# Attention with a gated dense branch: the gate, its product with the accumulator and the last additions on GpSimd, and 122 heads with V stationary

## The chip, the cores and the metric

The kernel runs on one core of a Trainium2 chip. The time is device microseconds of one execution; the median of the runs is what two kernels are compared by. A separate execution was recorded by the hardware profiler, and the profile page and every row below come from that one. The engines are called PE (TensorE matmuls), PEld (its weight loads), ACT (ScalarE), DVE (VectorE), POOL (GpSimd) and SP (SyncE, which only issues DMAs here).

## The reference

```python
def _A_ref(x, k_cache, v_cache, wq, wo):
    B, Sq, D = x.shape                     # 1, 2048, 512
    H, Dh = 32, 128
    q = (x @ wq).reshape(B, Sq, H, Dh).transpose(0, 2, 1, 3)
    scores = jnp.einsum("bhqd,bhkd->bhqk", q, k_cache) * (Dh ** -0.5)   # 2048 keys
    p = softmax(scores, axis=-1)
    o = jnp.einsum("bhqk,bhkd->bhqd", p, v_cache)
    return o.transpose(0, 2, 1, 3).reshape(B, Sq, H * Dh) @ wo
...
xn = layernorm(x)
s = A(xn)
g = silu(relu(xn @ w1 + b1) ** 2 @ w2 + b2)     # hidden width 1792
return x + s * g
```

Everything that enters and leaves is bf16.

## The kernel before, in words

The 2048 query rows are cut into four blocks `j` of 512 rows. A block has 32 heads, so there are 128 passes, called heads here and numbered `g` = 0 to 127. One head takes eight steps (`pi`); in each step PE makes two 128-key score tiles of 512 columns in PSUM (`psA`, two buffers), ACT takes their exponential into `pT` (one 128x1024 instruction, a ring of `NPT` = 8 buffers), and two steps later PE multiplies `pT` with V into `psO`.

There are two forms of that second product. **P stationary** (`gen_pv`, line 1004): `pT` is loaded as weights and V is streamed, with a column of ones beside it that yields the softmax denominator: 64 matmuls of 129 columns in a head. DVE copies the result out (`o_un`), POOL scales it (`o_bf`, line 1061), and a transposing DMA puts it into `oT`. **V stationary** (`gen_pv_b`, line 756): V is loaded as weights and `pT` is streamed: 16 matmuls of 512 columns. The result is already turned round; ACT copies it out (`o_col`), and the denominator has to be summed apart. For each of the eight tiles of a head either DVE reduces the whole 128x1024 tile (`den_part`, line 775), or POOL first adds its halves into `h_sum` (`part_add`, line 788) and DVE reduces the 128x512 sum (`part_half`, line 796). Then come a small sum, a turn, a DMA out and back (`d_scr`, `d_quad`), a small sum and a reciprocal, a DMA out and a broadcast back (`r_scr`, `r_all`), and POOL multiplies `o_col` with it into `oT` (`den_scale`, line 856). `at_a` (line 448) lists the heads with P stationary: the first `FIRST_B`, the last three and those in `A_HEADS`, together 11; the other 117 have V stationary.

Beside the heads PE works through jobs in the `psF` banks, spread evenly over the steps (`fill_one`): the projections of later heads (evicted as `qt_sb`), the dense branch (`job_h`, evicted as `r_t` and `h2T`; `job_o2`, line 1147), and the output projection in chunks of eight heads (`job_wo`, line 1186), whose first chunks are summed in `acc`. The gate of a tile of 128 rows is made in steps: DVE adds `b2` (`z_t`), ACT takes tanh (`th_t`), DVE makes (tanh + 1) * z (`g_all`, line 1166). Before the last chunk, DVE multiplies `acc` with the gate (`acc_gate`, line 1247) and POOL adds x (`acc_add`, line 1254). At the last chunk DVE multiplies its product by the gate into `tmp_t` (which is `z_t`, line 408), DVE adds `acc` to it, and POOL issues the store of the row tile.

A planner in the program fixes the order of each engine's instructions beforehand from estimated costs (`_cost`, line 60). Pieces of DVE work are queued in `quiet` by due step and put in where DVE is expected free (`fill_dve`, line 944); `pool_quiet` is the like for POOL: what is ready first goes first (`fill_pool`, line 961). POOL is also given a `part_add` where DVE owes more than `POOL_OWED` ns of queued work. The engines then run these orders and wait for each other by semaphores. Line numbers of the profile are those of the one-line helpers (line 226 is the plain matmul, 231 the one for P stationary, 239 `_tt`, 249 `_stt`, 286 the turning reduce). The two softmax buffers are joined by this rule in `gen_scores`, which makes ACT wait for the denominator work:

```python
deps=[t, t_PV[pi - NPT] if pi >= NPT else None, t_part.get(pi - NPT)])
```

Of the kernel before, what the change touches and what calls it, by code (L numbers as in the profile page):

```python
# [59 lines left out]
def _cost(name, fn):  # L60
    f, k = fn.func, fn.keywords
    n = _elements(k["out"])
    if name == "PE":
        return n / 2.4 + 2.5, n / 2.4 + 166
    if name == "ACT":
        return n * 0.83 + 70, n * 0.83 + 172
    if name == "POOL":
        if f is _tt and n > 1:
            c = n * 2.3 + 55 if k["out"].tensor.name == "oT" else n * 2.05 + 60
            return c, c + 50  # L70
        return (500, 560) if f is _tt else (n + 100, n + 150)
    if f is _reduce_t:
        n = _elements(k["in_"])
    elif f is _reduce:
        n = _elements(k["in_"]) * 1.3 + 35
    elif f is _recip:
        n = n * 3.1
    elif f in (_bn_stats,):
        n = _elements(k["in_"])
    elif f is _ts and _in_sbuf(k["in0"]):  # L80
        n = n / 2
    return n / 0.96 + 70, n / 0.96 + 150


def _uses_port(name, fn):
    f, k = fn.func, fn.keywords
    if name == "POOL":
        return f in (_tt, _ts)
    if name == "DVE":
        if f in (_tt, _stt):  # L90
            return _in_sbuf(k["in0"]) and _in_sbuf(k["in1"])
        if f in (_ts, _copy):
            return _in_sbuf(k.get("in0", k.get("in_")))
    return False
# [206 lines left out]
def bass_recurrent_scan__mha_block_cached__dense_activation_squared_relu__prompt_kernel(  # L301
# [37 lines left out]
    LATE_EVICT = 250  # L339
    POOL_ROOM = 300  # L340
    SLACK = 1500
    FIRST_B = 3
    A_HEADS = (10, 31, 41, 64, 96)
    POOL_OWED = 3500
    HALF_SLACK = 600
    VW = 136

# [31 lines left out]
    o_col = sb("o_col", [P, NOC, QB], F32)  # L379
    h_sum = sb("h_sum", [P, NHS, QB], F32)  # L380
    rden = sb("rden", [P, 2, TPB], F32)
    o_bf = sb("o_bf", [P, 2, TPB, Dh], BF16)
    NBK = QB // 32
    d_part = sb("d_part", [P, 2, 2 * NPR, NBK], F32)
    d_sum = sb("d_sum", [P, 2, 32], F32)
# [5 lines left out]
    r_scr = nc.dram_tensor("r_scr", [2, QB], F32, kind="Internal").ap()  # L391
    r_t = sb("r_t", [P, 2, QB], BF16)
    z_t = sb("z_t", [P, 2, D], F32)
    th_t = sb("th_t", [P, 1, D], BF16)
    b1b = sb("b1b", [NFC, P], BF16)
    b1f = sb("b1f", [P, NFC], F32)
    b2bc = sb("b2bc", [P, D], BF16)
# [492 lines left out]
    def needs(fn):  # L890
        f, a = fn.func, fn.args
        if f in (den_part, part_half):
            m = b_no[a[0] // NPR]
            if m >= 2 and m - 2 not in t_sum:
                return None
            return [t_exp[a[0]]] if f is den_part else [t_part[a[0]]]
        if f in (den_sum, den_turn, den_write, den_read, den_total, den_recip, rec_write,
                 rec_read, den_scale):
            g = a[0]
            m = b_no[g]  # L900
            if f is den_sum and tiles[g] < NPR:
                return None
            first, before = {
                den_sum: (t_parts.get(g, []), t_row), den_turn: ([t_sum.get(m)], t_dw),
                den_write: ([t_row.get(m)], t_dr), den_read: ([t_dw.get(m)], t_tot),
                den_total: ([t_dr.get(m)], t_rw), den_recip: ([t_tot.get(m)], {}),
                rec_write: ([t_rec.get(m)], t_spr), rec_read: ([t_rw.get(m)], t_scale),
                den_scale: ([t_col.get(m), t_spr.get(m)], {})}[f]
            if m >= 2 and f not in (den_recip, den_scale):
                first = first + [before.get(m - 2)]  # L910
            return first
        if f is norm_recip:
            return t_oev[a[0]]
        if f is norm_scale:
            return [t_rden.get(a_no[a[0]])]
        if f is acc_gate:
            return [t_acc[a[1]], t_g.get(a[0] * TPB + a[1])]
        if f is acc_add:
            jt = a[0] * TPB + a[1]
            return [t_ug.get(jt), tok_xt.get(jt)]  # L920
        if f is ln_bn:
            return [t_xl.get(a[0] * TPB + a[1])]
        if f is ln_rstd:
            return [t_bn.get(a[0] * TPB + a[1])]
        if f is ln_next:
            return [t_xr.get(a[0] * TPB + a[1])]
        return gate_needs[fn]

    def ready_at(fn):
# [131 lines left out]
    def norm_scale(g):  # L1061
        m = a_no[g]
        base = rden[:, m % 2, :]
        rb = bass.AP(tensor=base.tensor, offset=base.offset,
                     ap=[list(base.ap[0]), [1, TPB], [0, Dh]])
        t_norm[m] = t_onorm[g] = E(
            GP if g < NG - 3 else DV, partial(_tt, out=o_bf[:, m % 2, :, :], in0=o_un[:, :, 0:Dh], in1=rb, op=ALU.mult),
            deps=[t_rden[m], t_obf[m % 2]])
        gen_oT(g)

    def gen_oT(g):
        tok_oT[g] = t_obf[a_no[g] % 2] = S.emit_dma(
            SP, partial(_dmaT, out=oT[:, g % NOT, :].rearrange("p (t q) -> p t q", q=P),
                        in_=o_bf[:, a_no[g] % 2, :, :].rearrange("p t d -> p (t d)")), sl_oT[g % 4],
            deps=[t_onorm[g], t_wodone[g - NOT] if g >= NOT else None])


# [69 lines left out]
    def job_o2(j, qt):  # L1147
# [11 lines left out]
        def evac(bank, step):  # L1159
            s = jt % 2  # L1160
            assert jt < 1 or jt - 1 in t_g
            tz = E(DV, partial(_tt, out=z_t[:, s, :], in0=bankF(bank), in1=b2bc[:], op=ALU.add),
                   deps=[t_o2[j, qt], tok_b2, t_zrd[s], t_tmp[s]])
            box = [None]

            def gate():
                gs = jt % TPB
                t_g[jt] = t_zrd[s] = t_thr[0] = E(
                    DV, partial(_stt, out=g_all[:, gs, :], in0=th_t[:, 0, :], scalar=1.0,
                                in1=z_t[:, s, :], op0=ALU.add, op1=ALU.mult),  # L1170
                    deps=[box[0], t_fin.get(jt - TPB)])

            def tanh():
                box[0] = E(AC, partial(_act, out=th_t[:, 0, :], in_=z_t[:, s, :], func=ACT.Tanh,
                                       scale=0.5), deps=[tz, t_thr[0]])
                fn = partial(gate)
                gate_needs[fn] = [box[0]]
                calm(step + 8, fn)

            at(step + 1, tanh)  # L1180
            return tz
        return NFC, mm, evac

    t_fin = {}

    def job_wo(j, m, qt, c0=0, c1=D):
        jt = j * TPB + qt
# [15 lines left out]
        def evac(bank, step):  # L1203
# [2 lines left out]
                    t_wodone[j * H + h] = box[0]  # L1206
            place = (bankF(bank) if isinstance(bank, int) else bank[0])[:, 0:c1 - c0]
            if m == 0:
                t_acc[qt] = t = E(DV, partial(_copy, out=acc[:, qt, :], in_=place),
                                  deps=[box[0], t_fin.get(jt - TPB)])  # L1210
            elif not last:
                t_acc[qt] = t = E(DV, partial(_tt, out=acc[:, qt, :], in0=place,
                                              in1=acc[:, qt, :], op=ALU.add),
                                  deps=[box[0], t_acc[qt]])
            if m == len(CH[j]) - 2:
                calm(step + 16, partial(acc_gate, j, qt))
                pool_quiet.append(partial(acc_add, j, qt))
            if last:
                s = jt % 2
                assert all(x in t_g for x in t_o2j)  # L1220
                t = E(DV, partial(_stt, out=tmp_t[:, s, c0:c1], in0=place, scalar=0.5,
                                  in1=g_all[:, jt % TPB, c0:c1], op0=ALU.mult,
                                  op1=ALU.mult),
                      deps=[box[0], t_g[jt], t_tmp[s], t_zrd[s]])
                end = jt >= NQB * TPB - 2
                row = (x_t if end else out_t)[:, s, c0:c1]
                eng = GP if j == NQB - 1 and qt in (0, 2) else DV
                t_fin[jt] = t_tmp[s] = E(
                    eng, partial(_tt, out=row, in0=tmp_t[:, s, c0:c1],
                                 in1=acc[:, qt, c0:c1], op=ALU.add),  # L1230
                    deps=[t, t_u[jt], None if end else t_outdma[s]])
                eng, sl = (SP, sl_fin) if j == NQB - 1 else (GP, sl_out)
                dma = S.emit_dma(
                    eng, partial(_dma, out=out[0, jt * P:(jt + 1) * P, c0:c1],
                                 in_=row), sl[s], deps=[t_fin[jt]])
                if c1 == D:
                    t_outdma[s] = dma
            return t
        return nh, mm, evac

    def load_xt(jt):
        if jt < NQB * TPB:
# [3 lines left out]

    def acc_gate(j, qt):
        jt = j * TPB + qt
        t_ug[jt] = E(DV, partial(_stt, out=acc[:, qt, :], in0=acc[:, qt, :], scalar=0.5,
                                 in1=g_all[:, jt % TPB, :], op0=ALU.mult, op1=ALU.mult),  # L1250
                     deps=[t_acc[qt], t_g[jt]])


# [115 lines left out]
                                        in_=bass.AP(tensor=B_b2.tensor, offset=B_b2.offset,  # L1369
                                                    ap=[[0, P], [1, D]])), sl_b2)  # L1370

    at(62, load_b2)
    for i in range(2):
        at(140 + 8 * i, partial(load_xt, i))
    tok_w2 = None
# [175 lines left out]
```

The softmax here doesn't subtract the row's maximum and nothing guards it: scores larger than these inputs give would overflow.

## Time and profile before

| | before |
|---|---|
| median of 4 runs | 1219.08 us (1219.01 to 1220.62) |
| the profiled execution, own time | 1219.09 us |
| its span | 1217.3 us |
| PE busy | 1212.2 us, 100% of the span, 6269 matmuls |
| ACT busy | 1090.5 us, 90% |
| DVE busy | 1067.2 us, 88% |
| POOL busy | 1064.2 us, 87% |
| granted TensorE clock | 1.0 throughout |

The span runs from the first instruction to the last; the 1.8 us that are missing to the execution's own time lie around it. A row of the groups reads: line, engine, operation, output<-inputs, shapes and types, count | busy us, mean ns of one | idle time of the engine just before, and who ended it. Matmuls overlap in the profile, so the mean ns of one matmul is not what it adds; the distance from one start to the next is.

### The profile page before, as it was taken

Reading aid. Unit: us, or ns where it says so; the run is one execution under the profiler, and the core shown is the slowest. Engines: PE = TensorE matmul, PEld = TensorE weight load, DVE = VectorE, ACT = ScalarE, POOL = GpSimd, SP = SyncE. Lnnn points to the kernel's source line nnn. Section 1 sums busy time; section 2 is a strip of 40 time slices with the busy share of each in tenths; the row PEclk is TensorE's granted clock in tenths of the full one; section 3 lists DMA queues with packets and bytes.
Section 4 is the critical chain, followed back from the end, with each engine's and each line's share of the span. In section 5 each row is a group of like instructions: output and inputs, shape, how many; then the busy total and the mean of one; then the engine's idle time right before and its main releaser. Section 6 shows DMA issues by size and latency. Waiting matters only on the chain.

```text
span 1217.3 us, 19831 instructions
## 1 busy us (share of the span) xinstructions
PE 1212.2 (100%) x6269; PEld 667.7 (55%) x6269; DVE 1067.2 (88%) x1865; ACT 1090.5 (90%) x1162; POOL 1064.2 (87%) x982
## 2 busy tenths in 40 slices
PE   9999999999999999999999999999999999999999
PEld 7555555555555555555555555555555555555556
DVE  4798889899999898879999999888999999889973
ACT  7898989999899898999989999999999999989995
POOL 1687999999898899999888899999998889999981
PEclk9999999999999999999999999999999999999999
DMA  9889787878788776776777777877667777777771
GB/s 214 178 197 223 185 182 168 192 167 182 180 158 177 170 162 155 165 159 153 169 160 165 169 168 166 163 163 165 162 163 167 167 164 164 155 165 161 160 154 49
DMA packets 510009, 203.47 MB, mean 167 GB/s; under 512 B 421808, under 2 KB 493744, under 8 KB 509904
## 3 DMA queue, kind: packets, MB, share of 16 engines
q1 hardware_dynamic: 507808, 198.13, 75.0%
q0 software_dynamic: 1424, 3.81, 1.1%
q8 instruction: 50, 0.82, 0.3%
q14 instruction: 55, 0.45, 0.1%
q10 hardware_dynamic: 672, 0.26, 0.1%
HBM read 128.23 MB, written 4.25 MB: 109 GB/s over the span
## 4 chain that ended last, share of the span: by engine, by line
PE 96%; DVE 2%; POOL 1%; ACT 0%; DMA 0%; issue 0%; ACTq 0%
PE psA L226 36%; PE psO L226 32%; PE psF L226 25%; PE psO L231 3%; DVE d_part L286 1%; DVE acc L249 1%; POOL h_sum L239 0%; ACT pT L235 0%; PE psA L231 0%; DMA x_ln<-in_A_x_dram 0%; DVE qt_sb L253 0%; POOL oT L239 0%; POOL acc L239 0%; DVE acc L239 0%; ACT kT L235 0%
## 5 line engine op out<-in xcount | busy, mean ns | idle before, releaser
L235 ACT ACTIVATE pT<-psA 128x1024 bf16<-128x1024 f32 x1025 | 1036.6, 1025 | 108.3 <-PE psA L226 72.3
L239 POOL TENSOR_TENSOR h_sum<-pT 128x512 f32<-128x512 bf16 x758 | 863.0, 1166 | 63.0 <-DVE d_part L286 31.1
L226 PE MATMUL psA<-qt_sb,kT 128*128 128x512 bf16 x2032 | 605.4, 380 | 0.4 <-ACT pT L235 0.4
L226 PE MATMUL psO<-pT,v_sb 128*128 128x512 bf16 x1872 | 556.8, 379 | 0.0
L286 DVE TRANSPOSE_TENSOR_REDUCE d_part<-h_sum 128x16 f32<-128x512 f32 x758 | 495.3, 678 | 17.8 <-POOL h_sum L239 17.1
L226 PEld LDWEIGHTS psA<-qt_sb,kT 128*128 128x128 bf16 x2032 | 285.5, 144 | 179.2 <-ACT pT L235 4.5
L226 PEld LDWEIGHTS psO<-pT,v_sb 128*128 128x128 bf16 x1872 | 183.1, 98 | 220.1 <-issue 0.6
L286 DVE TRANSPOSE_TENSOR_REDUCE d_part<-pT 128x32 f32<-128x1024 bf16 x178 | 215.4, 1213 | 12.1 <-ACT pT L235 11.4
L226 PE MATMUL psF<-xnT,wq_sb 128*128 128x512 bf16 (+1 forms) x520 | 168.8, 374 | 0.2 <-DVE xnT L253 0.2
L226 PE MATMUL psF<-wo_all,oT 128*128 128x512 bf16 x480 | 163.7, 379 | 0.0
L239 POOL TENSOR_TENSOR oT<-o_col,r_all 128x512 bf16<-128x512 f32 x117 | 150.1, 1283 | 12.2 <-DMA r_all<-r_scr 12.0
L253 DVE CAST qt_sb<-psF 128x512 bf16<-128x512 f32 (+1 forms) x130 | 87.1, 670 | 32.4 <-PE psF L226 30.1
L226 PE MATMUL psF<-xnT,w_sb 128*128 128x512 bf16 x224 | 77.6, 379 | 0.0
L226 PEld LDWEIGHTS psF<-xnT,wq_sb 128*128 128x128 bf16 x520 | 50.3, 98 | 45.9 <-issue 0.3
L226 PE MATMUL psF<-w_sb,h2T 128*128 128x512 bf16 x224 | 73.8, 379 | 0.0
L235 ACT ACTIVATE o_col<-psO 128x512 f32<-128x512 f32 x117 | 69.3, 592 | 0.0
L226 PEld LDWEIGHTS psF<-wo_all,oT 128*128 128x128 bf16 x480 | 46.9, 98 | 40.1
L231 PEld LDWEIGHTS psO<-v_sb,pT 128*128 128x128 bf16 x704 | 46.6, 98 | 19.0 <-ACT pT L235 0.4
L245 DVE TENSOR_SCALAR r_t<-psF,b1f 128x512 bf16<-128x512 f32 x56 | 41.5, 741 | 16.9 <-PE psF L226 15.5
L231 PE MATMUL psO<-v_sb,pT 128*128 128x129 bf16 x704 | 54.0, 220 | 0.1
L282 DVE TENSOR_REDUCE d_sum<-d_part 128x16 f32<-128x144 f32 (+3 forms) x117 | 46.2, 395 | 1.3
L249 DVE SCALAR_TENSOR_TENSOR h2T<-psF,b1f,r_t 128x512 bf16<-128x512 f32 x56 | 41.8, 746 | 1.7
(66 smaller groups left out, 376.0 us busy)
## 6 DMA issues: line engine op xcount, KB each, us to landing
v_sb<-in_A_v_cache_dram SPq DMA_DIRECT2D x508, 128.0 KB, 2.7
r_all<-r_scr SPq DMA_DIRECT2D x117, 256.0 KB, 3.8
wq_sb<-in_A_wq_dram SPq DMA_DIRECT2D x127, 128.0 KB, 3.1
wo_all<-in_A_wo_dram SPq DMA_DIRECT2D x16, 256.0 KB, 3.6
kT<-in_A_k_cache_dram SPq DMA_TRANSPOSE x254, 3.6
w_sb<-in_B_w_dram SPq DMA_DIRECT2D x14, 256.0 KB, 3.5
x_t<-in_A_x_dram POOLq DMA_DIRECT2D x16, 128.0 KB, 3.0
d_scr<-d_row SPq DMA_DIRECT2D x117, 16.0 KB, 2.5
```

The source lines that it names most:

```text
L226: return e.matmul(out, lhsT, rhs, start=start, stop=stop)
L231: return e.matmul(out, lhsT, rhs, start=start, stop=stop, skip_group_check=True)
L235: return e.activation(out, in_, func, bias=bias, scale=scale)
L239: return e.tensor_tensor(out, in0, in1, op)
L245: return e.tensor_scalar(out, in0, scalar1=scalar1, scalar2=scalar2, op0=op0, op1=op1)
L249: return e.scalar_tensor_tensor(out=out, in0=in0, scalar=scalar, in1=in1, op0=op0, op1=op1)
L253: return e.tensor_copy(out, in_)
L282: return e.tensor_reduce(out, in_, axis=AX.X, op=ALU.add)
L286: return e.tensor_reduce(out, in_, axis=AX.X, op=ALU.add, apply_transpose=True)
```

## The change

Four things change. (1) The gate, its product with `acc`, and, outside the last block of rows, the addition of `acc` at the last chunk move from DVE to POOL and to its queue `pool_quiet`; the gate becomes two instructions. `finish` is new and also issues the store. (2) The factors 0.5 go: `z_t` is halved as it is made and `b2` once at the start; `th_t` becomes f32. (3) `FIRST_B` and `A_HEADS` change so that only heads 0, 1, 64 and the last three have P stationary: 6 of them, and 122 with V stationary. (4) `POOL_OWED` goes from 3500 to 4000, `o_bf` has one buffer, and the planner's costs know the new instructions.

```diff
--- before.py
+++ after.py
@@ -65,8 +65,8 @@
     if name == "ACT":
         return n * 0.83 + 70, n * 0.83 + 172
     if name == "POOL":
-        if f is _tt and n > 1:
-            c = n * 2.3 + 55 if k["out"].tensor.name == "oT" else n * 2.05 + 60
+        if f in (_tt, _stt) and n > 1:
+            c = n * 2.3 + 55 if k["out"].tensor.name in ("oT", "out_t") else n * 2.05 + 60
             return c, c + 50
         return (500, 560) if f is _tt else (n + 100, n + 150)
     if f is _reduce_t:
@@ -85,7 +85,7 @@
 def _uses_port(name, fn):
     f, k = fn.func, fn.keywords
     if name == "POOL":
-        return f in (_tt, _ts)
+        return f in (_tt, _ts, _stt)
     if name == "DVE":
         if f in (_tt, _stt):
             return _in_sbuf(k["in0"]) and _in_sbuf(k["in1"])
@@ -339,9 +339,9 @@
     LATE_EVICT = 250
     POOL_ROOM = 300
     SLACK = 1500
-    FIRST_B = 3
-    A_HEADS = (10, 31, 41, 64, 96)
-    POOL_OWED = 3500
+    FIRST_B = 2
+    A_HEADS = (64,)
+    POOL_OWED = 4000
     HALF_SLACK = 600
     VW = 136
 
@@ -379,7 +379,7 @@
     o_col = sb("o_col", [P, NOC, QB], F32)
     h_sum = sb("h_sum", [P, NHS, QB], F32)
     rden = sb("rden", [P, 2, TPB], F32)
-    o_bf = sb("o_bf", [P, 2, TPB, Dh], BF16)
+    o_bf = sb("o_bf", [P, 1, TPB, Dh], BF16)
     NBK = QB // 32
     d_part = sb("d_part", [P, 2, 2 * NPR, NBK], F32)
     d_sum = sb("d_sum", [P, 2, 32], F32)
@@ -391,7 +391,7 @@
     r_scr = nc.dram_tensor("r_scr", [2, QB], F32, kind="Internal").ap()
     r_t = sb("r_t", [P, 2, QB], BF16)
     z_t = sb("z_t", [P, 2, D], F32)
-    th_t = sb("th_t", [P, 1, D], BF16)
+    th_t = sb("th_t", [P, 1, D], F32)
     b1b = sb("b1b", [NFC, P], BF16)
     b1f = sb("b1f", [P, NFC], F32)
     b2bc = sb("b2bc", [P, D], BF16)
@@ -924,6 +924,9 @@
             return [t_bn.get(a[0] * TPB + a[1])]
         if f is ln_next:
             return [t_xr.get(a[0] * TPB + a[1])]
+        if f is finish:
+            jt = a[0]
+            return [fin_needs[fn], t_u.get(jt), t_outdma[jt % 2]]
         return gate_needs[fn]
 
     def ready_at(fn):
@@ -1064,14 +1067,14 @@
         rb = bass.AP(tensor=base.tensor, offset=base.offset,
                      ap=[list(base.ap[0]), [1, TPB], [0, Dh]])
         t_norm[m] = t_onorm[g] = E(
-            GP if g < NG - 3 else DV, partial(_tt, out=o_bf[:, m % 2, :, :], in0=o_un[:, :, 0:Dh], in1=rb, op=ALU.mult),
-            deps=[t_rden[m], t_obf[m % 2]])
+            GP if g < NG - 3 else DV, partial(_tt, out=o_bf[:, 0, :, :], in0=o_un[:, :, 0:Dh], in1=rb, op=ALU.mult),
+            deps=[t_rden[m], t_obf[0]])
         gen_oT(g)
 
     def gen_oT(g):
-        tok_oT[g] = t_obf[a_no[g] % 2] = S.emit_dma(
+        tok_oT[g] = t_obf[0] = S.emit_dma(
             SP, partial(_dmaT, out=oT[:, g % NOT, :].rearrange("p (t q) -> p t q", q=P),
-                        in_=o_bf[:, a_no[g] % 2, :, :].rearrange("p t d -> p (t d)")), sl_oT[g % 4],
+                        in_=o_bf[:, 0, :, :].rearrange("p t d -> p (t d)")), sl_oT[g % 4],
             deps=[t_onorm[g], t_wodone[g - NOT] if g >= NOT else None])
 
 
@@ -1159,29 +1162,36 @@
         def evac(bank, step):
             s = jt % 2
             assert jt < 1 or jt - 1 in t_g
-            tz = E(DV, partial(_tt, out=z_t[:, s, :], in0=bankF(bank), in1=b2bc[:], op=ALU.add),
+            assert jt < 2 or not {x for x in fin_due if x % 2 == s}
+            tz = E(DV, partial(_stt, out=z_t[:, s, :], in0=bankF(bank), scalar=0.5, in1=b2bc[:],
+                               op0=ALU.mult, op1=ALU.add),
                    deps=[t_o2[j, qt], tok_b2, t_zrd[s], t_tmp[s]])
             box = [None]
 
             def gate():
                 gs = jt % TPB
+                assert jt < TPB or jt - TPB in t_fin
+                t = E(GP, partial(_tt, out=th_t[:, 0, :], in0=th_t[:, 0, :], in1=z_t[:, s, :],
+                                  op=ALU.mult), deps=[box[0]])
                 t_g[jt] = t_zrd[s] = t_thr[0] = E(
-                    DV, partial(_stt, out=g_all[:, gs, :], in0=th_t[:, 0, :], scalar=1.0,
-                                in1=z_t[:, s, :], op0=ALU.add, op1=ALU.mult),
-                    deps=[box[0], t_fin.get(jt - TPB)])
+                    GP, partial(_tt, out=g_all[:, gs, :], in0=th_t[:, 0, :],
+                                in1=z_t[:, s, :], op=ALU.add),
+                    deps=[t, t_fin.get(jt - TPB)])
 
             def tanh():
-                box[0] = E(AC, partial(_act, out=th_t[:, 0, :], in_=z_t[:, s, :], func=ACT.Tanh,
-                                       scale=0.5), deps=[tz, t_thr[0]])
+                box[0] = E(AC, partial(_act, out=th_t[:, 0, :], in_=z_t[:, s, :], func=ACT.Tanh),
+                           deps=[tz, t_thr[0]])
                 fn = partial(gate)
                 gate_needs[fn] = [box[0]]
-                calm(step + 8, fn)
+                pool_quiet.append(fn)
 
             at(step + 1, tanh)
             return tz
         return NFC, mm, evac
 
     t_fin = {}
+    fin_due = set()
+    fin_needs = {}
 
     def job_wo(j, m, qt, c0=0, c1=D):
         jt = j * TPB + qt
@@ -1206,6 +1216,7 @@
                     t_wodone[j * H + h] = box[0]
             place = (bankF(bank) if isinstance(bank, int) else bank[0])[:, 0:c1 - c0]
             if m == 0:
+                assert jt < TPB or jt - TPB in t_fin
                 t_acc[qt] = t = E(DV, partial(_copy, out=acc[:, qt, :], in_=place),
                                   deps=[box[0], t_fin.get(jt - TPB)])
             elif not last:
@@ -1213,30 +1224,41 @@
                                               in1=acc[:, qt, :], op=ALU.add),
                                   deps=[box[0], t_acc[qt]])
             if m == len(CH[j]) - 2:
-                calm(step + 16, partial(acc_gate, j, qt))
+                pool_quiet.append(partial(acc_gate, j, qt))
                 pool_quiet.append(partial(acc_add, j, qt))
             if last:
                 s = jt % 2
                 assert all(x in t_g for x in t_o2j)
-                t = E(DV, partial(_stt, out=tmp_t[:, s, c0:c1], in0=place, scalar=0.5,
-                                  in1=g_all[:, jt % TPB, c0:c1], op0=ALU.mult,
-                                  op1=ALU.mult),
+                assert not {x for x in fin_due if x % 2 == s}
+                t = E(DV, partial(_tt, out=tmp_t[:, s, c0:c1], in0=place,
+                                  in1=g_all[:, jt % TPB, c0:c1], op=ALU.mult),
                       deps=[box[0], t_g[jt], t_tmp[s], t_zrd[s]])
-                end = jt >= NQB * TPB - 2
-                row = (x_t if end else out_t)[:, s, c0:c1]
-                eng = GP if j == NQB - 1 and qt in (0, 2) else DV
-                t_fin[jt] = t_tmp[s] = E(
-                    eng, partial(_tt, out=row, in0=tmp_t[:, s, c0:c1],
-                                 in1=acc[:, qt, c0:c1], op=ALU.add),
-                    deps=[t, t_u[jt], None if end else t_outdma[s]])
-                eng, sl = (SP, sl_fin) if j == NQB - 1 else (GP, sl_out)
-                dma = S.emit_dma(
-                    eng, partial(_dma, out=out[0, jt * P:(jt + 1) * P, c0:c1],
-                                 in_=row), sl[s], deps=[t_fin[jt]])
-                if c1 == D:
-                    t_outdma[s] = dma
+                fn = partial(finish, jt, c0, c1, t)
+                if j == NQB - 1:
+                    finish(jt, c0, c1, t)
+                else:
+                    fin_due.add(jt)
+                    fin_needs[fn] = t
+                    pool_quiet.append(fn)
             return t
         return nh, mm, evac
+
+    def finish(jt, c0, c1, t):
+        s = jt % 2
+        end = jt >= NQB * TPB - 2
+        row = (x_t if end else out_t)[:, s, c0:c1]
+        eng = DV if jt >= NQB * TPB - TPB and s else GP
+        t_fin[jt] = t_tmp[s] = E(
+            eng, partial(_tt, out=row, in0=tmp_t[:, s, c0:c1], in1=acc[:, jt % TPB, c0:c1],
+                         op=ALU.add),
+            deps=[t, t_u[jt], None if end else t_outdma[s]])
+        eng, sl = (SP, sl_fin) if jt >= NQB * TPB - TPB else (GP, sl_out)
+        dma = S.emit_dma(
+            eng, partial(_dma, out=out[0, jt * P:(jt + 1) * P, c0:c1], in_=row), sl[s],
+            deps=[t_fin[jt]])
+        if c1 == D:
+            t_outdma[s] = dma
+        fin_due.discard(jt)
 
     def load_xt(jt):
         if jt < NQB * TPB:
@@ -1246,8 +1268,8 @@
 
     def acc_gate(j, qt):
         jt = j * TPB + qt
-        t_ug[jt] = E(DV, partial(_stt, out=acc[:, qt, :], in0=acc[:, qt, :], scalar=0.5,
-                                 in1=g_all[:, jt % TPB, :], op0=ALU.mult, op1=ALU.mult),
+        t_ug[jt] = E(GP, partial(_tt, out=acc[:, qt, :], in0=acc[:, qt, :],
+                                 in1=g_all[:, jt % TPB, :], op=ALU.mult),
                      deps=[t_acc[qt], t_g[jt]])
 
 
@@ -1369,7 +1391,13 @@
                                         in_=bass.AP(tensor=B_b2.tensor, offset=B_b2.offset,
                                                     ap=[[0, P], [1, D]])), sl_b2)
 
-    at(62, load_b2)
+    def halve_b2():
+        nonlocal tok_b2
+        tok_b2 = E(DV, partial(_ts, out=b2bc[:], in0=b2bc[:], scalar1=0.5, scalar2=None,
+                               op0=ALU.mult), deps=[tok_b2])
+
+    at(58, load_b2)
+    at(66, halve_b2)
     for i in range(2):
         at(140 + 8 * i, partial(load_xt, i))
     tok_w2 = None
```

## The prediction

> **What bounds the kernel now.** I read the page from the chain that ended last, then the stages, then the waits. The chain gives PE 96%; the stages say whether PE is full everywhere.
>
> ```profile
> PE 96%; DVE 2%; POOL 1%; ACT 0%; DMA 0%; issue 0%; ACTq 0%
> ```
>
> Busy time of each engine in stretches (the columns are the stretch, its length, then busy us of PE, PEld, DVE, ACT, POOL, with instructions in brackets):
>
> ```profile
> 60.00:90.00 30.00, 30.00 (x141) 15.97 (x139) 28.60 (x52) 27.33 (x29) 26.92 (x26) 1.00 0.89 197
> 600.00:630.00 30.00, 29.57 (x183) 17.13 (x182) 28.77 (x46) 25.78 (x28) 24.21 (x23) 1.00 0.74 158
> 990.00:1020.00 30.00, 30.00 (x141) 15.99 (x139) 28.98 (x54) 27.32 (x30) 26.43 (x25) 1.00 0.69 158
> ```
>
> From 30 to 1200 us PE is busy without a hole in every 30 us stretch except 600:630, which lacks 0.43 us. It does 140 to 141 matmuls of 512 columns in 30 us, so 0.2155 us each (696 in the 150 us from 630 to 780). The middle of this kernel can only get shorter if PE gets less to do or loses that 0.43 us. DVE at 29.0 of 30 and POOL at 26.4 cost PE nothing: they matter only where they make ACT or PE wait. The one hole, in order of time:
>
> ```profile
> 604.48 2.52 DVE L249 SCALAR_TENSOR_TENSOR acc<-acc,g_all 128x512 f32<-128x512 f32 x1
> ...
> 607.07 1.16 POOL L239 TENSOR_TENSOR acc<-acc,x_t 128x512 f32<-128x512 f32 x1 [0.63 <-DVE acc L249]
> ...
> 609.12 3.38 POOL L239 TENSOR_TENSOR h_sum<-pT 128x512 f32<-128x512 bf16 x3
> ...
> 614.93 3.05 ACT L235 ACTIVATE pT<-psA 128x1024 bf16<-128x1024 f32 x3 [1.21 <-POOL h_sum L239]
> ...
> 616.01 0.66 PE L226 MATMUL psA<-qt_sb,kT 128*128 128x512 bf16 x2 [0.43 <-ACT pT L235]
> ```
>
> DVE's product with the gate takes 2.52 us, POOL's addition waits for it, the `h_sum` pieces come late, ACT finds no free `pT` for 1.21 us, and PE loses 0.43.
>
> **The change, part by part.** The sum is made against the profiled execution's 1219.09 us, which is the median of the runs (1219.08) as well.
>
> *Five heads (2, 10, 31, 41, 96) go to V stationary.* PE: in the timeline eight 129-column matmuls take from 304.48 to 304.94, 306.70 to 307.15 and 308.02 to 308.48 until the next group starts: 0.455 us. A head has eight such groups: 3.64 us. With V stationary it is 16 x 0.2155 = 3.45. Five heads: 5 x 0.19 = **-0.95 us**, all on the path. ACT gains 5 copies of `o_col` at 0.592 = 3.0 us; it idles 72.3 us waiting for PE, so this is hidden. Without that cover it would cost up to 3.0. SP gains 20 small DMA issues and loses 5 transposes; the waits show no PE instruction held by a DMA, not even in 90:120 where the DMA engines are 0.99 busy: nothing (bounds: 0, and 1 us if head 2's chain held up an early load).
>
> *POOL.* The rows:
>
> ```profile
> L239 POOL TENSOR_TENSOR acc<-acc,x_t 128x512 f32<-128x512 f32 x16 | 18.5, 1156 | 8.1 <-DVE acc L249 8.1
> L239 POOL TENSOR_TENSOR x_t<-z_t,acc 128x512 bf16<-128x512 f32 x1 | 1.3, 1271 | 1.2 <-DVE z_t L249 1.2
> L294 POOL DMA_DIRECT2D out_dram<-out_t x12 | 7.0, 582 | 21.2 <-DVE out_t L239 21.2
> L249 DVE SCALAR_TENSOR_TENSOR acc<-acc,g_all 128x512 f32<-128x512 f32 x16 | 29.6, 1850 | 0.0
> L249 DVE SCALAR_TENSOR_TENSOR g_all<-th_t,z_t 128x512 bf16<-128x512 bf16 x16 | 16.7, 1047 | 0.0
> ```
>
> Added: 16 `acc` x gate at 1.156 (f32 and bf16 in, as `acc_add`) = 18.5; 16 gate additions (two f32 in, bf16 out, as the second row) at 1.27 = 20.3; 16 tanh x z with three f32 tiles, which the trace does not show: between 1.156 and 1.283 (the `oT` group), I take 1.22 = 19.5; 12 additions outside the last block at 1.27 = 15.2. Together 73.5 us. Each of 44 pairs waits for POOL's own result, 0.3 us as `x_t` issued after `acc` shows (3.9 us in 13): 13.2. Five heads: 5 x 1.283 for `oT` less 5 x 1.04 for `o_bf`: +1.2. Removed is idling: 21.2 us in which POOL stood before a store for DVE's addition, and 8.1 before `acc_add`. Net 58.6 us, as much as 50 `h_sum` additions of 1.166, which I expect POOL to hand back to DVE: some 710 instead of 758.
>
> *DVE.* Removed: 29.6 + 16.7 + 12 x 0.735 = 55.1 us, and 5.0 for the copies and reciprocals of five heads. Added: 5 denominator chains at 0.395 + 0.191 + 0.215 + 0.221 = 5.1; 40 new tiles as whole reductions at 1.213 = 48.5; 50 tiles back, each 1.213 - 0.678: 26.8; halving `b2` once, 0.3 to 0.7. Net +21: 1067 to about **1088 us**, 89% of the span. That is less than the 28.6 to 29.0 of 30 which DVE holds for 100 us at a time without harm, so off the path: 0. If the cover were gone, DVE's late evictions of `psF` would stop PE.
>
> The trade looks poor by the rows: the DVE product has a minimum of 0.647 us and takes 1.156 on POOL. The Trainium skill speaks against it too: in "GPSIMD Engine Reference", section 4.1, elementwise work belongs on VectorE, GpSimd being about twice as slow with two inputs. That page's 4497 ns for 2048 elements would make 1.12 us of each instruction (an estimate, a quarter), so 60 x 1.12 = 67 us where the rows give 73.5. But the DVE rows here are 1.85 and 1.05 us in the mean, with maxima of 3.04 and 2.94, against minima of 0.647 and 0.616: DVE loses 26 us beside POOL on work that needs about 20. "SBUF — State Buffer", section "Who interferes with whom", says that a DVE instruction with two SBUF inputs and a GpSimd one that reads SBUF lock each other out; by it DVE waits for one POOL instruction, here it waited up to 2.4 us, two of them.
>
> *The hole at 616.* Its first step, the 2.52 us on DVE, is gone: **-0.43**. What is late next is POOL's pair `acc` x gate, then plus x: 2.3 us and 0.3 in place of 1.16 and 0.63. It can be paid back (bounds -0.43 and +0.43); I take the gain, since DVE is free meanwhile to empty `h_sum`.
>
> *New waits.* DVE's writes to `z_t`, and its first copy to `acc`, now wait for POOL's `finish` or gate of an earlier tile; behind them stand the `psF` evictions, and PE behind those. The rows give the distance: additions at 377.2 and 386.7, two buffers, so 19 us; gates 17 us or more (`z_t` at 466.6 and 484.3). ACT's tanh waits for the gate before, with the exponentials behind it: 17 us as well. POOL took up its additions to `acc` at most 2.2 us after the product before them (575.1 to 577.3), so nothing; with POOL 17 us late each would cost what it is late. With one `o_bf`, heads 126 and 127 wait for a DMA that is issued 7 us before (1189.3, 1197.8) and lands in 2.5: nothing. The last tile's gate, near 1180, becomes 4.8 us on POOL where its next `oT` pieces come after 2.07 and 4.53 us of idling: nothing. The end after 1200 keeps its instructions.
>
> Sum: 1219.09 - 0.95 - 0.43 = **1217.7 us**, 0.11% below. About 0.2% (2.4 us) is what a measurement of this kernel can tell from no change, so this is "the same".
>
> **Rivals.**
>
> *POOL comes late and ACT waits (slower).* There are 44 pairs of POOL instructions of 2.3 to 2.5 us, ahead of the `h_sum` additions that free `pT`. For it: the waits show ACT held by POOL's `h_sum` 9 times (3.4 us) and by `oT` twice, and POOL is 27.8 to 30.0 of 30 busy from 120 to 300 us. Against it: of the 13 times ACT waited for POOL or DVE all but the two near 609 and 615 cost PE under 0.1 us, and ACT has 2.5 us in 30 to catch up. Price: 0.43 for a pair as at 616. From 1217.7 it takes nine such pairs to reach 1221.5, where "slower" begins; the 12 of `acc` outside the last block would give 1222.9, all 44 would give 1236.6. Most likely place: where `acc` and `finish` cluster, 270 to 400, 570 to 690, 870 to 1000 us. Chance 0.21; likely 1221.6 to 1224.
>
> *The gain is given back (same).* Two to eight such holes: 1218.6 to 1221.1. For it: without heads 10, 31, 41 and 96 nothing relieves DVE and POOL in the dense stage. Against it: from 626 to 905 us no such head comes and PE loses under 0.1 us. Chance 0.14.
>
> *Faster by over 0.2%.* PE would have to lose 2.4 us of work or waiting; beyond 0.95 and 0.86 (all start delays near 605 to 617) only the first 16 us, which the change leaves, hold 3.6 us. Time 1216.4 at best. Chance 0.05.
>
> *POOL does not hand the additions back*, and DVE falls below 1067 while POOL passes 1100. PE is full either way: 1217.7 again, part of the forecast.
>
> **Numbers.** Forecast (with the last rival) 0.60, between 1217.1 and 1218.6; given back 0.14; slower 0.21; faster 0.05. Faster 0.05, same 0.74, slower 0.21. The range leaves out 0.05 below and 0.12 above: 1216.8 to 1222.8.
>
> **What would show it.** Right: PE 6029 matmuls (5 x 48 fewer), 30.00 of 30 in every middle stretch; no POOL wait for `out_t`; DVE's two gate groups gone; `h_sum` 690 to 730; DVE 1070 to 1100. Wrong: PE waits for ACT `pT` in the clusters with ACT waiting for POOL, DVE above 29 of 30 with PE below 30, or PE held by a load near 40 to 60 us.

## The result, and the profile after

The changed kernel takes 1217.57 us (median of 34 runs, 1217.23 to 1218.12); the kernel before took 1219.31 us in the same series (median of 54 runs): 1.7 us less, against a forecast of 1217.7. The ratio on record is 0.9982, 95% interval 0.9977 to 0.9987 (the two medians alone give 0.9986), so the gain is clear of noise although it is under the 0.2% that the prediction took for the limit. Of the 54 runs before 33 lie between 1218.99 and 1219.60 us, 20 between 1220.58 and 1221.11, and one stands alone at 5984.87; against the median of the first group the gain is 1.6 us. The execution that was profiled took 1218.07 us, its span 1216.3.

The chain and the first part of the page, of the changed kernel:

```profile
PE 1211.6 (100%) x6029; PEld 659.7 (54%) x6029; DVE 1075.4 (88%) x1867; ACT 1092.5 (90%) x1167; POOL 1114.2 (92%) x1025
...
PE 99%; ACT 0%; DMA 0%; DVE 0%; POOL 0%; issue 0%; ACTq 0%
```

The same three stretches (stretch, length, then busy us of PE, PEld, DVE, ACT, POOL):

```profile
60.00:90.00 30.00, 30.00 (x141) 16.01 (x139) 28.48 (x52) 27.34 (x29) 28.59 (x27) 1.00 0.97 190
600.00:630.00 30.00, 30.00 (x188) 17.59 (x187) 25.71 (x45) 26.92 (x30) 23.86 (x23) 1.00 0.81 172
990.00:1020.00 30.00, 30.00 (x141) 16.01 (x139) 28.11 (x49) 27.55 (x30) 28.30 (x27) 1.00 0.69 165
```

PE has 240 matmuls fewer, five heads' difference of 48 each, and the stretch from 600 to 630 us is full. The 2% that DVE had in the chain, the stretch before the hole, is gone. Of the groups, the additions into `h_sum` before the change:

```profile
L239 POOL TENSOR_TENSOR h_sum<-pT 128x512 f32<-128x512 bf16 x758 | 863.0, 1166 | 63.0 <-DVE d_part L286 31.1 <-ACT pT L235 24.6 <-DVE d_rec L282 2.5
```

and after it, with the denominator work of DVE and the moved work:

```profile
L239 POOL TENSOR_TENSOR h_sum<-pT 128x512 f32<-128x512 bf16 x746 | 841.6, 1158 | 44.0 <-DVE d_part L286 19.9 <-ACT pT L235 15.6 <-DVE d_rec L257 3.5
L286 DVE TRANSPOSE_TENSOR_REDUCE d_part<-pT 128x32 f32<-128x1024 bf16 x230 | 276.9, 1211 | 10.0 <-ACT pT L235 9.4
L239 POOL TENSOR_TENSOR th_t<-th_t,z_t 128x512 f32<-128x512 f32 x16 | 20.4, 1276 | 0.0
L239 POOL TENSOR_TENSOR g_all<-th_t,z_t 128x512 bf16<-128x512 f32 x16 | 20.4, 1275 | 1.3
L239 POOL TENSOR_TENSOR acc<-acc,g_all 128x512 f32<-128x512 f32 x16 | 18.5, 1157 | 0.1
L294 POOL DMA_DIRECT2D out_dram<-out_t x12 | 7.0, 581 | 3.6 <-POOL out_t L239 3.3 <-DVE d_row L290 0.3
```

POOL no longer idles 21 us before the stores (3.6 is left), and its busy time rose by 50 us, since, in the balance, it handed back only 12 of the additions into `h_sum` (746 against 758).

The spans of the two profiled executions differ by only 1.0 us because this one started 0.6 us later (its first load of x took 3.22 us in the chain, 2.75 before) and took 0.3 us more after its last matmul. From the first 512-column score matmul to the end of the last matmul it is 1198.1 us before (16.6 to 1214.7) and 1196.2 after (17.2 to 1213.4), 1.9 us less. This stretch, called the matmul stretch below, leaves out the start, which differs from trace to trace by up to 0.7 us; it is the better measure for differences of a few tenths.

### The profile page after: what moved, and what is told of

It is laid out like the page before. It is cut to its first block, busy times and chain, and to the rows that moved or that the text cites. A ratio compares the mean times of both kernels' runs of the same rounds, so it can differ in the third digit from the quotient of the medians.

```text
span 1216.3 us, 19405 instructions
## 1 busy us (share of the span) xinstructions
PE 1211.6 (100%) x6029; PEld 659.7 (54%) x6029; DVE 1075.4 (88%) x1867; ACT 1092.5 (90%) x1167; POOL 1114.2 (92%) x1025
## 4 chain that ended last, share of the span: by engine, by line
PE 99%; ACT 0%; DMA 0%; DVE 0%; POOL 0%; issue 0%; ACTq 0%
PE psA L226 37%; PE psO L226 35%; PE psF L226 25%; PE psO L231 2%; PE psA L231 0%; DMA x_ln<-in_A_x_dram 0%; ACT pT L235 0%; PE psF L270 0%; ACT kT L235 0%; DVE st_t L274 0%; POOL rstd L239 0%; ACTq L208 0%; PE psO L270 0%; DVE xnT L253 0%; DVE xn_t L245 0%
## 5 line engine op out<-in xcount | busy, mean ns | idle before, releaser
L239 POOL TENSOR_TENSOR h_sum<-pT 128x512 f32<-128x512 bf16 x746 | 841.6, 1158 | 44.0 <-DVE d_part L286 19.9
L226 PE MATMUL psO<-pT,v_sb 128*128 128x512 bf16 x1952 | 580.6, 379 | 0.0
L286 DVE TRANSPOSE_TENSOR_REDUCE d_part<-h_sum 128x16 f32<-128x512 f32 x746 | 488.6, 679 | 19.0 <-POOL h_sum L239 18.2
L226 PEld LDWEIGHTS psA<-qt_sb,kT 128*128 128x128 bf16 x2032 | 288.7, 144 | 186.1 <-ACT pT L235 3.6
L226 PEld LDWEIGHTS psO<-pT,v_sb 128*128 128x128 bf16 x1952 | 191.0, 98 | 229.5
L286 DVE TRANSPOSE_TENSOR_REDUCE d_part<-pT 128x32 f32<-128x1024 bf16 x230 | 276.9, 1211 | 10.0 <-ACT pT L235 9.4
L239 POOL TENSOR_TENSOR oT<-o_col,r_all 128x512 bf16<-128x512 f32 x122 | 155.9, 1278 | 10.0 <-DMA r_all<-r_scr 9.9
L253 DVE CAST qt_sb<-psF 128x512 bf16<-128x512 f32 (+1 forms) x130 | 87.2, 671 | 29.2 <-PE psF L226 27.1
L282 DVE TENSOR_REDUCE d_sum<-d_part 128x16 f32<-128x160 f32 (+4 forms) x122 | 49.8, 408 | 2.1
L226 PEld LDWEIGHTS psF<-w_sb,h2T 128*128 128x128 bf16 x224 | 21.9, 98 | 19.4
L226 PEld LDWEIGHTS psF<-xnT,w_sb 128*128 128x128 bf16 x224 | 21.9, 98 | 18.6
```

Source lines behind the costliest of these rows:

```text
L226: return e.matmul(out, lhsT, rhs, start=start, stop=stop)
L239: return e.tensor_tensor(out, in0, in1, op)
L253: return e.tensor_copy(out, in_)
L282: return e.tensor_reduce(out, in_, axis=AX.X, op=ALU.add)
L286: return e.tensor_reduce(out, in_, axis=AX.X, op=ALU.add, apply_transpose=True)
```

## The experiments

Each was run beside the kernel before on the same chip; the ratios are to that kernel. The first four shared its runs (median 1219.26 us), the second four (1219.21), and the last four (1219.16). The three sets and the changed kernel were not all run together, so where a run is compared with the changed kernel by its median, a few tenths of a microsecond say little; the matmul stretch of its trace is given too where they matter. In the four traces of the second set 2% of the matmul records are missing (5914 of 6029). One is missing every 10.8 us and leaves 0.05 us of idle time on PE, so PE's busy time is not read from those traces; a hole of 0.3 us or more stands out.

**The heads alone.** In the kernel before:

```diff
-    FIRST_B = 3
-    A_HEADS = (10, 31, 41, 64, 96)
+    FIRST_B = 2
+    A_HEADS = (64,)
```

> The kernel before with only the heads moved (FIRST_B 2, A_HEADS 64 alone); gate, product and additions stay on DVE. Theory (PE's own work decides): five heads fewer at 0.19 us, so 0.95 us below the kernel before, ratio 0.9992, if DVE's slack of 12% covers the 40 new tiles. Rival (the five heads were the relief that DVE and POOL needed, and the move to POOL is what makes them dispensable): DVE above 29 of 30 in the dense stages, PE under 30 of 30 in several stretches, ACT waiting for POOL or DVE for more than 6 us in all, ratio 1.000 or above.

1221.62 us, ratio 1.0019 (1.0010 to 1.0028): 2.4 us slower. The rival held. Two stretches, and the product, which stays on DVE here:

```profile
300.00:330.00 30.00, 29.56 (x136) 15.13 (x135) 29.76 (x49) 26.25 (x28) 27.32 (x25) 1.00 0.72 173
330.00:360.00 30.00, 29.06 (x134) 15.09 (x133) 29.29 (x52) 25.80 (x28) 25.43 (x23) 1.00 0.62 142
```

```profile
L249 DVE SCALAR_TENSOR_TENSOR acc<-acc,g_all 128x512 f32<-128x512 f32 x16 | 26.5, 1659 | 0.0
```

DVE is at 29.3 to 29.8 of 30, and PE lacks 0.4 and 0.9 us; 2.6 us in all over five stretches between 180 and 990 us. Idle time is not the whole loss: the matmul stretch is 1200.5 us, 4.3 more than in the changed kernel, and the late starts on PE add up to as much. ACT waits 7.6 us for `h_sum` (15 times) where the kernel before had 3.4 (9 times).

**The moves alone.** In the changed kernel:

```diff
-    FIRST_B = 2
-    A_HEADS = (64,)
+    FIRST_B = 3
+    A_HEADS = (10, 31, 41, 64, 96)
```

> The changed kernel with the heads of before (FIRST_B 3, A_HEADS 10, 31, 41, 64, 96): only the work of DVE moves. Theory: 0.95 us above the changed kernel, so about 0.4 to 0.8 us below the kernel before (the hole near 616 gone), ratio 0.9993 to 0.9997. Rival (the moves alone bring the whole gain): ratio 0.9982 as the changed kernel. Second rival (moving work to the slower engine costs by itself): ratio above 1.000, ACT waiting for POOL more than in the kernel before.

1218.32 us, ratio 0.9992 (0.9983 to 1.0000): 0.94 us below the kernel before and 0.75 above the changed one. That is the theory, with a little more gain than the 0.8 us that it allowed. In the matmul stretch (1197.3 us) it is 0.8 below the kernel before and 1.1 above the changed one. No start of a matmul in the middle is over 0.1 us late.

**Nineteen heads more with P stationary.** In the changed kernel `A_HEADS = tuple(range(6, 121, 6))`: twenty heads in place of head 64.

> The changed kernel with every sixth head from 6 to 120 with P stationary, 25 in all in place of 6. Theory (0.19 us of PE for each such head, 57 ns for a matmul of 129 columns): 19 x 0.19 = 3.6 us above the changed kernel, about 1221.2 us, ratio to the kernel before 1.0015. Rival (only the columns count, 64 x 129 against 16 x 512, 27 ns a head): 0.5 us above, 1218.1 us, ratio 0.9987. Second rival (the relief of DVE and POOL pays): at or below the changed kernel.

1221.72 us, ratio 1.0019 (1.0010 to 1.0028): 4.15 us above the changed kernel for 19 heads, 0.22 us each (0.23 by the matmul stretch). DVE falls to 79% and POOL to 81%, and nothing is won by it: PE's own work decides. The rival by columns is out.

**Without head 64.** In the changed kernel `A_HEADS = ()`.

> The changed kernel without head 64 with P stationary: 123 heads with V stationary. Theory: 0.19 us less, 1217.4 us, ratio to the kernel before 0.9980, PE 30.00 of 30 throughout the middle. Rival (the one relief in the middle is needed): PE waits for ACT near 580 to 700 us, ratio at or above 0.9985.

1217.35 us, ratio 0.9984 (0.9975 to 0.9993), 0.22 below the changed kernel. That is the theory's number, but not its reason: one start near 655 us is 0.35 us late, more than the 0.2 that the head is worth, and the matmul stretch is 1196.4 us against 1196.2. The lower median doesn't come from the head. The rival's hole did appear, in one place.

**The product back on DVE.** In the changed kernel:

```diff
-                pool_quiet.append(partial(acc_gate, j, qt))
+                calm(step + 16, partial(acc_gate, j, qt))
...
-        t_ug[jt] = E(GP, partial(_tt, out=acc[:, qt, :], in0=acc[:, qt, :],
+        t_ug[jt] = E(DV, partial(_tt, out=acc[:, qt, :], in0=acc[:, qt, :],
```

> The changed kernel with one part undone: the product of acc with the gate goes back to DVE, in its queue by due step; gate and additions stay on POOL. Theory (the long DVE instructions that wait beside POOL are what made tiles late): product of 1.6 us or more in the mean, ACT waiting for POOL or DVE more than 5.3 us in all, holes near 300 to 360 or 930 to 980, 1218.0 to 1219.5 us, ratio 0.9990 to 1.0002. Rival (this part does nothing, the gate itself or the additions do): 1217.5 to 1217.8 us, ratio 0.9983 to 0.9986.

1219.96 us, ratio 1.0005 (0.9996 to 1.0015), 2.4 above the changed kernel and 0.5 above the range that was expected. The instructions take 1.88 us in the mean:

```profile
L239 DVE TENSOR_TENSOR acc<-acc,g_all x16: 616/1649/4264, 272.7 to 1182.1; 128x512 f32<-128x512 f32 x16
```

(minimum, median and maximum in ns). ACT waits 9.6 us for POOL and DVE before its exponentials (18 times), against 4.1 in the changed kernel. The chain to the largest hole, at 602 us, starts with a product that took 3.42 us (the chain counts 3.36 of it):

```profile
593.92 3.36 DVE acc L239
597.28 0.60 DVE qt_sb L253
597.88 2.94 DVE d_part L286 x4
...
600.90 1.03 ACT pT L235
...
601.98 0.66 PE psA L226 x2
```

PE idles 0.87 us there, and 0.53 at 617 and 0.30 at 312 us, each with a product in its chain (1.36 and 4.19 us).

**The additions back on DVE.** In the changed kernel `finish` is called at once for every tile, and its addition is done by DVE except for two of the last block, as in the kernel before.

> The changed kernel with one part undone: the last additions outside the last block go back to DVE, at once after the product, and POOL waits for each before it issues the store (about 21 us of idling for 12 stores). Theory (PE has cover in ACT, and POOL hands tiles back): at most one or two holes of 0.43 us, 1217.5 to 1218.4 us, ratio 0.9983 to 0.9991. Rival (POOL's idling before the stores is what costs): above 1218.8 us, ACT waiting for POOL near 340 to 400, 650 to 690, 950 to 1000.

1218.58 us, ratio 0.9992 (0.9982 to 1.0001): 1.0 us above the changed kernel, between the two theories' figures. On DVE the additions are hardly stretched (0.73 us in the mean), while POOL idles 20.0 us before its stores: that idling costs something, but under half of the product.

**A DVE instruction with one input in place of the product.** In the kernel of the heads alone:

```diff
-        t_ug[jt] = E(DV, partial(_stt, out=acc[:, qt, :], in0=acc[:, qt, :], scalar=0.5,
-                                 in1=g_all[:, jt % TPB, :], op0=ALU.mult, op1=ALU.mult),
+        t_ug[jt] = E(DV, partial(_bn_stats, out=idle6[:, 0:6], in_=acc[:, qt, :]),
```

> The kernel before with only the heads moved, and acc_gate replaced by a DVE statistics instruction over acc alone, of the same planned cost, with one SBUF input: the product of acc with the gate is left out. Theory (DVE is blocked beside POOL when both its inputs are in SBUF, and this blocking makes the holes): the replacement takes 0.65 to 0.70 us where the product took 1.66, DVE loses 16 us of busy time, holes fall from 2.6 us of missing PE time in the 30 us stretches to under 1.3, time 1218.5 to 1220.3. Rival (too many instructions on DVE, not the blocking): holes stay, 1221 us or more. Second rival (any DVE instruction is slowed beside POOL): replacement above 1.0 us.

1217.85 us, ratio 0.9988 (0.9979 to 0.9997): 3.8 us below the kernel of the heads alone, and below the lower end of what was expected.

```profile
L274 DVE BATCH_NORM_STATS2 idle<-acc 128x6 f32<-128x512 f32 x16 | 10.5, 654 | 0.1
```

The product is left out, so this kernel doesn't compute the reference. DVE has as many instructions as in the run with the heads alone (1910), and POOL about as much to add (780 `h_sum` against 782); the blocking of the product is gone, 0.65 us in place of 1.66, 16 us in all. It is not the only difference: the planner, which counts conflicts beside POOL (`_uses_port`), chose another order, with the seventh of the 16 at 593.9 us in place of 603.4. One hole is left, 0.43 us at 199 us, which the run with the heads alone has too. The chain to it starts with a gate on DVE, blocked for 4.7 us:

```profile
183.90 4.62 DVE g_all L249
188.52 4.65 DVE d_part L286 x6
...
198.38 0.92 ACT pT L235
...
199.35 0.65 PE psA L226 x2
```

In the run with the heads alone the chains to the holes at 316 and 936 us go through products of 2.4 and 2.8 us, those to the holes at 346, 354 and 974 us through none.

**POOL first.** In the changed kernel `POOL_OWED = 0`.

> The changed kernel with POOL_OWED 0 in place of 4000: POOL takes a tile's first addition whenever it can. It tests the rival of the prediction that POOL comes late. Theory (POOL at its limit makes tiles late, ACT waits, PE follows at about 0.43 us a hole): h_sum above 830, POOL above 96% in the middle stretches, DVE below 1030 us, ACT waiting for POOL above 8 us, 1218.5 to 1223 us, ratio 0.9991 to 1.003. Rival (DVE was the tight engine, and more on POOL is harmless): 1217.3 to 1217.8 us, ratio 0.998 to 0.9986.

1217.60 us, ratio 0.9982 (0.9973 to 0.9992): no difference. It tells nothing of either theory, because the knob does next to nothing here:

```profile
L239 POOL TENSOR_TENSOR h_sum<-pT 128x512 f32<-128x512 bf16 x748 | 843.6, 1158 | 43.2 <-DVE d_part L286 19.7 <-ACT pT L235 14.8 <-DVE d_rec L257 3.6
```

748 additions against 746: POOL already takes nearly every tile it finds time for. So the step from 3500 to 4000 in the change, which lies in this range, should matter little; it was not run by itself.

**The gate back on DVE**, as one instruction, in the kernel of the moves alone. It was not run with the changed kernel's heads.

> The kernel of the moves alone (heads of before, product and additions on POOL), with the gate back on DVE as one instruction. Theory (blocking of DVE instructions with two SBUF inputs makes holes only where the work is dense; the gates lie 17 us or more apart): gate 1.0 to 1.4 us in the mean on DVE, no hole over 0.1 us or one, 1218.2 to 1218.8 us, ratio 0.9991 to 0.9997. Rival (the gate's move is worth as much as the product's): above 1219.2 us.

1218.62 us, ratio 0.9994 (0.9985 to 1.0003), 0.3 us above the moves alone. The gate took 1.14 us in the mean on DVE and made no hole, and the matmul stretch is the same in both (1197.3 us), so the 0.3 doesn't come from the gate. With these heads its move is worth nothing; with the changed kernel's heads a blocked gate did lead to a hole, the one at 199 us above.

**Two and four products more on POOL.** In the changed kernel, after the product:

```diff
+        for _ in range(2):
+            t_ug[jt] = E(GP, partial(_tt, out=acc[:, qt, :], in0=acc[:, qt, :],
+                                     in1=g_all[:, jt % TPB, :], op=ALU.mult), deps=[t_ug[jt]])
```

> The changed kernel, with acc multiplied by the gate two more times on POOL in each of the 16 places, so that POOL's block there is 4.6 us and not 2.3. It asks how long a block POOL may put ahead of the tiles. Theory (a tile has about 8 steps of 1.17 us from its exponential to the one that wants its buffer, and POOL hands tiles to DVE): ACT waits for POOL 4 to 10 us in all, 0 to 4 holes, 1217.6 to 1219.3 us. Rival (POOL late stops ACT at once, 0.43 us for each of the 12 blocks outside the last rows and more): 1222 us or more. Second rival (no effect): 1217.4 to 1217.7.

The product is then made three times, and five times in the second run, so neither computes the reference; they only load POOL. With two more, 1222.69 us, ratio 1.0028 (1.0018 to 1.0039): 5.1 us above the changed kernel. The rival's time held, 0.3 us in the mean for each of the 16 longer blocks, but not its picture of a loss at every block. The stretches in which PE isn't full, and the waits of ACT:

```profile
600.00:630.00 30.00, 27.56 (x173) 15.89 (x172) 25.26 (x41) 23.78 (x26) 23.90 (x22) 1.00 0.68 141
...
900.00:930.00 30.00, 29.28 (x136) 15.43 (x135) 27.07 (x42) 26.62 (x29) 29.07 (x27) 1.00 0.72 161
930.00:960.00 30.00, 29.07 (x135) 14.94 (x133) 28.88 (x53) 25.84 (x28) 27.33 (x25) 1.00 0.71 156
```

```profile
ACT pT L235 <- POOL h_sum L239: 9.4, 19, 1.8
ACT pT L235 <- DVE d_part L286: 4.0, 5, 2.1
```

(waited for: us, times, longest). The holes stand in and after two of the clusters of products, near 600 and 900 us, and DVE is not full in them: 25.3 and 27.1 of 30 in the first two stretches. The clusters near 300 and 1150 us have none.

> As the run with two more products, but four more, POOL's block 6.9 us in each of 16 places, 74 us of POOL's time more in all. Theory: the cover of about 9 us from exponential to reuse, less the work already queued, is used up in the clusters: holes near 300 to 400, 580 to 690, 880 to 1000, DVE above 29 of 30 there, 1219.5 to 1228 us. Rival (POOL hands everything to DVE in time): below 1218.5 us.

With four more, 1228.65 us, ratio 1.0076 (1.0064 to 1.0089), 11.1 us above the changed kernel and a little over what was expected: twice the extra work, twice the loss.

**No head in the middle, and `POOL_OWED` 5000.** `A_HEADS = ()` and `POOL_OWED = 5000` in the changed kernel.

> 123 heads with V stationary (head 64 too) and POOL_OWED 5000, a version meant to beat both kernels. Theory (PE's work alone if the hole of 0.35 us near 654 of the run with POOL_OWED 4000 closes): 1217.0 us, ratio 0.9981; if the hole stays 1217.35. Rival (less given to POOL leaves DVE short): 1218 us or more.

1217.31 us (1217.00 to 1217.74), ratio 0.9984 (0.9975 to 0.9993). The hole near 655 us is closed:

```profile
630.00:660.00 30.00, 30.00 (x141) 16.01 (x140) 29.63 (x52) 27.50 (x30) 28.70 (x27) 1.00 0.72 170
```

It has 123 heads with V stationary. Its median is 0.26 us below the changed kernel's, and its matmul stretch (1195.9 us) is 0.3 below: about the 0.2 us that one head is worth. Against the run without head 64 the stretch is 0.45 us shorter, as the closed hole promised, though the medians are alike. The ratios (0.9984 here, 0.9982 for the changed kernel) don't tell the two apart.

## Why the prediction was right, point by point

- **The time.** The forecast of 1217.7 us came within 0.1 us of the median, and the mechanism named was the right one, but the closeness is in part luck. The two terms, 1.38 us, are 0.5 short of the 1.9 in the matmul stretch; the start and a median of the kernel before that lay 0.2 above the prediction's 1219.09 made up for most of that.
- **Five heads, -0.95 us.** From the moves alone to the changed kernel it was 0.75 by the medians and 1.1 by the matmul stretch; the nineteen heads give 0.22 for each, 1.09 for five. The price per head was right. But the step holds only on top of the moves: on the kernel before, the same five heads cost 2.4 us. The prediction added the two parts as if each stood alone. Its rival "the gain is given back" names the relief that these heads gave, but no term prices the heads without the moves. Shown: -0.95 became +2.4 without them, and the difference, 3.1 to 3.5 us, is what the moves protect.
- **The hole at 616, -0.43 us.** The mis-sized term: the moves alone gave 0.94 by the medians, 0.84 in the matmul stretch. The page's 0.43 counts only idle time after the modelled end of the last matmul. By starts, PE was 0.59 us late at 616.01 (the eight matmuls from 614.97 need 0.455) and 0.15 late at 610.51 (two from 609.93 need 0.43), with smaller ones 0.86 in all, a figure that the prediction named among its rivals and did not use in the sum.
- **Moving the work to the slower engine pays.** Right, and for the reason weighed there. Of what was moved, the product is worth most (2.4 us by the medians), then the additions (1.0); the gate nothing where it was tried. The chains show how the blocking makes a hole: DVE stands in one instruction for 1.4 to 4.6 us, what is behind it comes late, ACT finds no free `pT`, and PE waits. They show it for the hole before, at 616, for the three with the product back on DVE, and for three of the six larger ones with the heads alone; for the other three it is not shown. The run with the one-input instruction has as many DVE instructions and one hole left, so their number alone doesn't make the holes; it leaves the product out and has another order, so it is not a clean price of the blocking. The Trainium skill's rule in "SBUF — State Buffer", "Who interferes with whom", that a DVE instruction with at most one SBUF input, outside the modes that use both ports, doesn't contend with GpSimd, agrees here: 0.654 us in the mean, 0.695 at most, beside a POOL that is 89% busy.
- **POOL.** Instruction prices were right (1.157, and 1.275 where I took 1.22 and 1.27). The forecast of 710 additions was not: POOL kept 746, and DVE came to 1075 us where I had 1088. Three terms account for most of that. A pair in which POOL waits for its own result costs 0.08 us (1.3 us in 16), not 0.3, which is what a DMA issue waits, so these waits came to some 5 us and not 13.2. Each `h_sum` addition fell from 1.166 to 1.158 us, 6 us over all. The largest was put at nothing: POOL idled 19 us less before its additions into `h_sum` (44.0 where it was 63.0), and 9 less before `o_bf`, which fewer heads need. With 36 of the 48 additions kept that I expected back on DVE, POOL (1114 us) came nearer to the rival that it hands nothing back; PE was full either way, as that rival said.
- **DVE at 29.0 of 30 without harm, so 0.** True of this kernel, but too loose as a reason: in the run of the heads alone DVE at 29.3 to 29.8 went with holes, in the last version 29.63 went without, and with two more products the largest hole stands in a stretch with 25.3. The share doesn't decide; in the chains of these runs it is long work ahead of a tile that is nearly due.
- **New waits, 0.** Right: no wait of DVE or ACT for `finish` or the gate is in the trace.
- **The slower rival, POOL late.** It did not happen, but its mechanism is real and near: 2.3 us more in POOL's blocks cost 5.1 us. Its price, 0.43 a block, was not far from the 0.3 that the longer blocks cost in the mean.

The shorter `h_sum` additions can be traced: before, 19 of the 758 took over 1.23 us (1.85 at most), and 18 of these ran beside a gate (12) or a product (6) on DVE; after, none did. Without these 19 the mean before is 1.156 us. Not shown: what the gate alone is worth with the changed kernel's heads.

## What to carry to other kernels

Where one engine is full, a change elsewhere is worth only the holes that it opens or closes, and these are read from the starts of that engine's instructions, not from its idle time. Work may be cheaper on an engine that takes nearly twice as long, if on the faster one it stands blocked in a queue that others wait for; look at minimum and mean of its duration. Parts of a change are not terms of a sum when one is the cover of the other: price each one without the rest.

## What the runs showed of the hardware that was not expected

- The product on DVE, with both inputs in SBUF, took from 0.62 us to 4.26 us (mean 1.88) beside POOL when it was put back. The longest on record is a gate of 4.70 us in the run of the heads alone (4.71 in that with the one-input instruction), from 183.8 us on, while POOL ran four instructions one after the other (183.3 to 187.9): DVE can stand through more than one. POOL is held up as well, but less: its `h_sum` additions took 1.85 us at most before the change, and 1.16 nearly always.
- A DVE instruction with one bf16 tile in and out is stretched as well: the layernorm scaling took 0.40 to 0.41 us on the four tiles of the first 13 us, where POOL hardly works, and up to 1.36 us later in the changed kernel (0.832 in the mean of its group; 0.697 before, 0.941 with the heads alone). The f32 statistics with one input were not (0.654).
- Two POOL instructions of which one reads the other's result follow each other within 0.08 us; a DMA that POOL issues after its own result starts 0.3 us later (3.3 us in 11).
